# GpSimd scaling of the pooled attention weights, single sums of q and k, and a halved last store in a fused attention and two-layer kernel

## The chip, the cores and the metric

The kernel runs on one core of one Trainium2 chip. A core has five engines with a queue of instructions each: TensorE (PE in the profile, with its weight loads as PEld), VectorE (DVE), ScalarE (ACT), GpSimd (POOL) and SyncE (SP), which here issues all the DMAs. The metric is the time of one execution on the device, in microseconds (us); lower is better.

## The reference

```
# attention, q k v: (4 batches, 8 heads, 576 positions, 64)
q_d, k_d, v_d = means over 4 neighbouring positions            # 144 positions
out_d  = softmax(q_d k_d^T / 8) v_d, each row repeated 4 times  # pooled part
scores = q k^T / 8, kept where |i - j| < 4                      # local part, 7 wide
out    = out_d + softmax(scores) v
x = out as (2304 tokens, 512)
h = x @ w_in;  g = max(h, 0) + alpha * min(h, 0);  x = g @ w_out        # 512 -> 2048 -> 512
h = x @ w_in2; g = where(h > 0, h, exp(min(h, 0)) - 1); y = g @ w_out2  # 512 -> 2048 -> 512
```

All of it is in float32, and the weights of both layers come as float64 bits that the kernel decodes.

## The kernel before

**Tiling.** Two heads make a pair `p`, so a batch `b` has four. Half a batch (288 tokens) is a group, `g` or `u`. The first layer runs over groups and over 16 slices `f` of 128 hidden channels, numbered `s`: `mm_in` multiplies slice `f` of `w_in` (tile `wi`), `th_elem` applies the activation (tiles `n`, `r`, then a high half `gh` and a low half `gl`), and `out1` multiplies by `w_out` (`wo`) into four banks of PSUM. Except in the first six slices, a float32 product is made from three products of high and low halves: the high half of a weight is an ACT copy, the low half a DVE subtraction into the same tile (`raw_l`, `raw_d`). Before that, ACT and DVE decode the bits (`raw_a`, `raw_b`; tiles `cp`, `rawi`, `rawo`, `cw`). The second layer has the same parts in a Strassen form; `th_fin2` adds its last partial sums (tile `os`) and stores rows of 128 tokens.

**Attention of batch 0** comes first, since the first layer needs its output. For each pair: `sums_qk` sums q and k over four positions on DVE, `sums_v` does it for v on POOL (tile `vh`); `sd_mm` forms the pooled scores, `sd_max`, `sd_exp` and `sd_rec` the softmax (tile `P`, row sums `dsum`), `sd_norm` scales `P` by one over the row sums, `pt_mm` and `pt_ev` transpose it, `dav_mm` multiplies by v. The local part is `th_dense` and `th_soft0` (tiles `Dmx`, `Dden`, `dP`; `d_mm` makes the scores, `d_av` multiplies by v), once for each half `u`. `p_add` adds the two into `x`, and when pair `p` of half 0 is there, `mm_first` can multiply its quarter of the sum over 512 channels. While it waits for a quarter of slice 0, it may take the quarters that are there for slices 1 up to `EB` - 1.

**Attention of batches 1 to 3** is spread between the slices of the first layer. `load_qk` brings q and k of a pair, `s_mm` forms the scores of a block (20 blocks, 2 heads), `s_ev` and `s_write` bring them to DRAM (`ss`, `scr`), and once all pairs are written, `s_read` reads the band (`sd`) and `softmax_a` and `softmax_b` run on DVE.

**What sets the order.** The order on each engine is fixed at build time: threads of Python generators (`th_...`) yield what they wait for, each with a priority (`VP`, `DP`, `NP0`, `US`, `OX` and others; a lower one goes first), and a clock inside the program (`_Clock`) decides which one records its next instruction. Where that clock sees TensorE without work, `run_while` records a small multiplication of ones (tile `warm`). So a change of a cost or a priority moves instructions of many other threads. `yield ("DVE",)` hands the turn to other threads until the clock's DVE is near. All instructions are recorded by a helper at L326, so that rows of the profile are told apart by their tiles.

Of the kernel before, what the change touches and what calls it, by code (L numbers as in the profile page):

```python
# [7 lines left out]
F32 = mybir.dt.float32  # L8
# [5 lines left out]
ALU = mybir.AluOpType  # L14
AX = mybir.AxisListType
# [3 lines left out]
S = 576  # L19
D = 64  # L20
NP = H // 2
DM = H * D
# [11 lines left out]
HALO = 3  # L34
# [3 lines left out]
SD = S // 4  # L38
# [7 lines left out]
ZK = 7  # L46
LO = 2
VP = -15.5
DP = -14.5
NP0 = -14.95  # L50
STEP = 1.0
TC = 105
# [2 lines left out]
U2 = G2 // 2  # L55
XR = 11
DN = 1
BIAS = -9000.0
NP2 = NF // 2
WARM = True  # L60
# [16 lines left out]
OSD = 12  # L77
OSO = -4
OAV = 12
OX = -5  # L80
UD = -11
US = -10
UG = (("xcp",3),("xcp",3),("xc",0,0),("xc",0,0))
EB = 2
PSX = 1
PV = 1
VTM = 1
# [243 lines left out]
def fused_kernel(ctx: ExitStack, tc: tile.TileContext, qk, vt, vk, vl, ql, kl, w_in1, w_out1, alpha,  # L331
# [3 lines left out]
    PE, ACT, DVE, SP, POOL = (_Engine(n, e, ck) for n, e in  # L335
                              (("PE", nc.tensor), ("ACT", nc.scalar), ("DVE", nc.vector), ("SP", nc.sync),
                               ("POOL", nc.gpsimd)))
# [7 lines left out]
    accb, hb = bank[0:4], bank[4:6]  # L345
# [15 lines left out]
    osp = dram.tile([NTOK, DM], F32, name="osp")  # L361
# [6 lines left out]
    Ap = pA.__enter__()  # L368

    assert w_in1.dtype == U64  # L370
    WS = 2.0 ** -8
# [110 lines left out]
    st = {}  # L482
# [120 lines left out]
    def sums_qk(b, p):  # L603
        if b:
            sm = Ap.tile([128, 2 if VTM else 3, SD], F32, tag="sm", name="sm", bufs=2)
        else:
            sm = st["qk", 0, p][1][:, SP_:].rearrange("p (a c) -> p a c", a=3)
        st["sm", b, p] = sm
        for a in range(2):
            DVE.tensor_reduce(out=sm[:, a, :],  # L610
                              in_=st["qk", b, p][a][:, HALO:HALO + S].rearrange("p (c f) -> p c f", f=4),
                              axis=AX.X, op=ALU.add)

    def sums_v(b, p):
        if not b and PV:
# [148 lines left out]

    def sd_norm(key, dve):
        P, sm = st[("P",) + key], st.pop(("ds",) + key)
        for r in range(2):
            for i in range(len(key[2])):
                if dve:
                    DVE.tensor_scalar(out=P[:, r, i], in0=P[:, r, i], scalar1=sm[:, r, i], scalar2=None, op0=ALU.mult)  # L770
                else:
                    ACT.activation(out=P[:, r, i], in_=P[:, r, i], func=AF.Copy, scale=sm[:, r, i])
# [101 lines left out]
    NJ = NF // 4  # L874
    NB2 = -(-NTOK // G2)
    HALF = NB2 - 1
    turns = [(1, 0), (2, 1), (0, 2), (3, 3), (1, 4), (HALF, 4), (2, 5), (0, 6), (3, 7), (HALF, 8)]
# [3 lines left out]
    size = [min(G2, NTOK - z * G2) for z in range(NB2)]  # L881
# [23 lines left out]
    def spawn(gen, pri, start=-1, lim=LIM, early=EARLY):  # L905
        threads.append({"g": gen, "p": pri, "s": start, "c": ck.ctx(), "w": None, "l": lim, "e": early})
        threads.sort(key=lambda t: t["p"])

    def finish(*key):
        done[key] = ck.cur["t"]  # L910
# [237 lines left out]
    def th_pair(b, p):  # L1148
        if b:
            if b == 1:  # L1150
                yield "key", *GATE
            yield "tok", "qk"
            yield "tok", "vv"
            yield ("DMA",)
            load_qk(b, p)
            finish("ld", b, p)
            load_v(b, p)
        else:
            yield "key", "ld0", p, 1
        if b:  # L1160
            yield "tok", "sm"
        yield ("DVE",)
        sums_qk(b, p)
        finish("sq", b, p)
        if not b:
            yield "key", "ldv", p
        if b and VTM:
            yield "tok", "vs"
        yield ("DVE",) if b or not PV else ("POOL",)
        sums_v(b, p)  # L1170
        finish("sv", b, p)
        if b:
            put("vv")
            if VTM:
                finish("vs", b, p)
                yield from th_da(b, p, (0, 1))
                return
            yield "tok", "vs"
        bks = yield "bank", 1
        vT_mm(b, p, bks[0])  # L1180
        if not b:
            finish("vT", p)
        yield ("ACT",)
        vT_ev(b, p, bks[0])
        release(bks)
        finish("vs", b, p)
        if b:
            yield from th_da(b, p, (0, 1))

    def th_da(b, p, qs):  # L1190
        key = (b, p, qs)
        yield "tok", "P"
        bks = yield "bank", 2, 1
        sd_mm(b, p, qs, bks)
        if b:
            put("sm")
        if b or not PSX:
            yield ("ACT",)
            sd_ev(key, bks)
            release(bks)  # L1200
            bks = None
        yield ("DVE",)
        sd_max(key, bks)
        yield ("ACT",)
        sd_exp(key, bks)
        if bks:
            release(bks)
        yield ("DVE",)
        sd_rec(key)
        yield ("DVE",) if b < DN else ("ACT",)  # L1210
        sd_norm(key, b < DN)
        yield "tok", "pt"
        bks = yield "bank", 2
        pt_mm(key, bks)
        put("P")
        yield ("ACT",)
        pt_ev(key, bks)
        release(bks)
        if b in QUAD:
            finish("pt", b, p)  # L1220
            return
        yield "key", "vs", b, p
        if b and SPR:
            bks = yield "spare", 1
        else:
            bks = yield "bank", 1
        dav_mm(key, bks[0])
        put("pt")
        if b:
            put("vs")  # L1230
        else:
            finish("dav", p, qs)
        yield ("ACT",)
        dav_ev(key, bks[0])
        (unspare if b and SPR else release)(bks)
        finish("od1", b, p, qs)
        if all(("od1", b, z, qs) in done for z in range(NP)):
            finish("od", b, qs[-1])
# [595 lines left out]
    def down2(u, f):  # L1834
        i, j = divmod(u, NJ)
        z, wq = turns[i]
        wq += j
        run_until("gu", u, f)
        run_until("wo", wq, f)
        gh, gl = gs["u", u]  # L1840
        W2 = st["Wo", wq, f]
        t = [done["gu", u, f], done["wo", wq, f]]
        for m in range(size[z] // 128):
            if not j and not f:
                last = i - 1 if not i or m < size[turns[i - 1][0]] // 128 else i - 2
                run_until("fin2", last, m)
                t.append(done["fin2", last, m])
            at(*t)
            c = f * size[z] + m * 128
            for k, (g, pw) in enumerate(((gh, "h"), (gh, "l"), (gl, "h"))):  # L1850
                PE.matmul(out=accb[m], lhsT=g[:, c:c + 128], rhs=W2[:, HL[pw]],
                          start=(not j and not f and k == 0), stop=(j == NJ - 1 and f == 1 and k == 2))
            if j == NJ - 1 and f:
                spawn(th_fin2(i, m), -101)
            tick()
        if lastv[wq] == i:
            ck.cur["t"] = ck.t["PE"]
            finish("fr", wq // NJ + 1, wslot[wq % NJ][4 + f])
# [9 lines left out]
            st["os", i, m] = t  # L1868
            finish("os", i, m)

    def th_fin2(i, m):
        z, h = turns[i][0], again[i]
        r0 = z * G2 + m * 128
        ck.cur["t"] = ck.t["PE"]
        if h:
            yield "key", "os", i, m
            t = st.pop(("os", i, m))
            yield ("DVE",)
            DVE.scalar_tensor_tensor(out=t, in0=accb[m], scalar=WS, in1=t, op0=ALU.mult, op1=ALU.add)
        else:  # L1880
            yield "tok", "os"
            yield ("ACT",) if m % 2 else ("DVE",)
            t = cp["pool"].tile([128, DM], F32, tag="os", name="os", bufs=4)
            if m % 2:
                ACT.activation(out=t, in_=accb[m], func=AF.Copy, scale=WS)
            else:
                DVE.tensor_scalar(out=t, in0=accb[m], scalar1=WS, scalar2=None, op0=ALU.mult)
        finish("fin2", i, m)
        SP.dma_start(out=(out if h else osp)[r0:r0 + 128, :], in_=t)
        put("os")  # L1890
        if not h:
            finish("part", z, m)
        if all(("fin2", i, k) in done for k in range(size[z] // 128)):
            finish("fin2", i)

    ring = [0]

    with tc.manual_schedule():
        cp["pool"], cp["cw"] = Ap, 2
# [3 lines left out]
        for step in LORD.split():  # L1903
            p = int(step[1:] or 0)
# [27 lines left out]
        for b in range(1, B):  # L1932
            g0 = 32 * (b - 1)
            for z in range(NP):
                p = QORD[z] if b in QUAD else z
# [13 lines left out]
            for u in range(2):  # L1949
                spawn(th_vl(b, u), g0 + 5 + u)  # L1950
                spawn(th_av(b, u), g0 + OAV + 16 * u, -1, LS)
                for i in range(HT // TS):
                    spawn(th_x(b, u, i), g0 + 16 * u + OX + i / 10)
        at(4000.0)
        DVE.tensor_scalar(out=nal, in0=nal, scalar1=-1.0, scalar2=1.0, op0=ALU.mult, op1=ALU.add)
        for s in range(NS1):
            slot[0] = s if s else -1
            ly, g, f, first, last, i = seq[s]
# [3 lines left out]
            if s == TC:  # L1962
# [7 lines left out]
                for q in range(NQ):  # L1970
                    p = 2 + max(0, q - NJ + 1) + q / 100
# [10 lines left out]
            key = (ly, "i", f)  # L1982
            wk = ("w32" if s < F1 else "w", key)
            run_until(*wk)
            if s < F1:
                t = 0.0
            else:
                run_until("xc", *segs[i][4:6])
                t = tm["x"]
# [25 lines left out]
            while len(pend) > LAG or (last and len(pend) > 1) or (first and not seq[pend[0]][5] == i):  # L2015
                z = pend.pop(0)
# [2 lines left out]
                sync()  # L2019
        for m in range(4):  # L2020
            done["fin2", -1, m] = 0.0
        NU2 = len(turns) * NJ
        for u in range(NU2):
            slot[0] = NS1 + u
            i, j = divmod(u, NJ)
# [108 lines left out]
```

## Time and profile before

| | |
|---|---|
| median of 3 runs | 890.29 us (888.11 to 893.06) |
| the profiled execution | 887.87 us |
| its span, first to last instruction | 886.10 us |
| PE busy | 874.3 us, 6631 instructions |
| DVE, ACT, POOL busy | 743.9, 544.9, 4.8 us |
| mean granted clock of TensorE | 0.998 of full speed |

The profiled execution lies 2.42 us below the median, and 1.77 us of it lie outside the span. TensorE is busy nearly throughout, so what counts is the time in which it is idle, runs multiplications of ones, or runs at the lower clock.

### The profile page before, as it was taken

The numbers are of one execution on the slowest core, as the hardware profiler recorded it, in microseconds if no ns is written. First come the engines' busy times: TensorE is split into PE (matmuls) and PEld (weight loads), VectorE is DVE, ScalarE is ACT, GpSimd is POOL, SyncE is SP. The second block draws the span as 40 slices with busy tenths as digits, with TensorE's granted clock in tenths as the row PEclk, the third lists the DMA queues.
The fourth block names the chain that finished last, engine by engine and source line by source line (L and its number), as shares of the span: only waits on it lengthen the run. The fifth ranks groups of instructions, "written<-read, shape, count | busy, mean of one in ns | idle before, by whom it ended". The sixth has DMA issues, their size and how long they took to land.

```text
span 886.1 us, 17496 instructions
## 1 busy us (share of the span) xinstructions
PE 874.3 (99%) x6631; PEld 812.9 (92%) x6631; DVE 743.9 (84%) x1618; ACT 544.9 (61%) x1436; POOL 4.8 (1%) x12
## 2 busy tenths in 40 slices
PE   8999999999999999999999999999999999999998
PEld 6679889999999999999999999999999899999987
DVE  6999899898899989998676999979796669887952
ACT  6899887893447734344365776756565556656643
POOL 2000000000000000000000000000000000000000
PEclk9999999999999999999999999999999999999999
DMA  9958813603405132011402814141414064250501
GB/s 315 344 186 232 256 22 108 187 17 103 126 5 173 41 93 69 1 56 45 163 28 95 265 49 170 48 166 51 141 48 143 2 217 132 83 190 25 191 26 71
DMA packets 67716, 103.80 MB, mean 117 GB/s; under 512 B 26784, under 2 KB 43424, under 8 KB 67632
## 3 DMA queue, kind: packets, MB, share of 16 engines
q1 hardware_dynamic: 67632, 102.68, 36.4%
q8 instruction: 52, 0.85, 0.4%
q14 instruction: 32, 0.26, 0.1%
HBM read 84.75 MB, written 17.92 MB: 116 GB/s over the span
## 4 chain that ended last, share of the span: by engine, by line
PE 87%; DVE 5%; ACT 4%; DMA 2%; issue 1%; SPq 0%; ACTq 0%; DVEq 0%
PE bank L326 87%; ACT P L326 1%; ACT dP L326 1%; DMA rawi<-in_w_in_dram 1%; DMA qk<-in_qk_dram 1%; DVE gl L326 0%; DVE qk L326 0%; ACT cp L326 0%; DMA ident<-in_ident_dram 0%; SPq L326 0%; DVE n L326 0%; DVE wi L326 0%; DVE acc L326 0%; DVE r L326 0%; DMA out_dram<-os 0%
## 5 line engine op out<-in xcount | busy, mean ns | idle before, releaser
L326 PE MATMUL bank<-gh,wo 128*128 128x288 f32 x976 | 221.6, 299 | 0.0
L326 PE MATMUL bank<-xh,wi 128*128 128x288 f32 x976 | 218.3, 298 | 2.0 <-DVE wi L326 2.0
L326 PEld LDWEIGHTS bank<-xq,wi 128*128 128x128 f32 x1536 | 194.4, 191 | 6.1
L326 PE MATMUL bank<-xq,wi 128*128 128x256 f32 x1536 | 196.4, 283 | 0.0
L326 ACT ACTIVATE n<-bank 128x288 f32<-128x288 f32 (+1 forms) x176 | 70.3, 400 | 184.5 <-PE bank L326 179.7
L326 PE MATMUL bank<-wo,gh 128*128 128x512 f32 x576 | 179.3, 392 | 0.0
L326 PEld LDWEIGHTS bank<-xh,wi 128*128 128x128 f32 x976 | 164.2, 189 | 4.4 <-DVE wi L326 2.2
L326 PEld LDWEIGHTS bank<-gh,wo 128*128 128x128 f32 x976 | 165.6, 189 | 2.4 <-issue 2.1
L326 PE MATMUL bank<-gl,wo 128*128 128x288 f32 x488 | 145.3, 298 | 0.2 <-DVE gl L326 0.2
L326 PE MATMUL bank<-xl,wi 128*128 128x288 f32 x488 | 144.2, 295 | 0.0
L326 PEld LDWEIGHTS bank<-wo,gh 128*128 128x128 f32 x576 | 103.1, 189 | 17.5
L326 PE MATMUL bank<-wo,gl 128*128 128x512 f32 x288 | 112.4, 390 | 0.8 <-DVE gl L326 0.7
L326 PEld LDWEIGHTS bank<-gl,wo 128*128 128x128 f32 x488 | 92.2, 189 | 0.5 <-DVE gl L326 0.4
L326 PEld LDWEIGHTS bank<-xl,wi 128*128 128x128 f32 x488 | 92.4, 189 | 0.1
L326 ACT ACTIVATE gh<-r 128x288 fp32r<-128x288 f32 x122 | 53.9, 442 | 54.0 <-DVE r L326 53.5
L326 DVE SCALAR_TENSOR_TENSOR r<-n,nal,bank 128x288 f32<-128x288 f32 x128 | 64.9, 508 | 22.1 <-ACT n L326 21.7
L326 PEld LDWEIGHTS bank<-wo,gl 128*128 128x128 f32 x288 | 54.1, 188 | 13.6 <-DVE gl L326 1.8
L326 DVE TENSOR_TENSOR gl<-r,gh 128x288 fp32r<-128x288 f32 x122 | 55.0, 452 | 8.2 <-ACT gh L326 7.7
L326 DVE TENSOR_TENSOR gl<-n,gh 128x512 fp32r<-128x512 f32 (+1 forms) x80 | 50.2, 633 | 7.1 <-ACT gh L326 6.0
L326 DVE TENSOR_TENSOR c<-m,bank 128x256 f32<-128x256 f32 x64 | 26.3, 418 | 35.1 <-PE bank L326 34.7
L326 ACT ACTIVATE gh<-n 128x512 fp32r<-128x512 f32 (+1 forms) x80 | 46.1, 582 | 13.2 <-DVE n L326 12.9
L326 ACT ACTIVATE n<-n 128x512 f32<-128x512 f32 (+1 forms) x80 | 47.2, 589 | 2.5
(123 smaller groups left out, 1225.3 us busy)
## 6 DMA issues: line engine op xcount, KB each, us to landing
rawo<-in_w_out_dram SPq DMA_DIRECT2D x38, 512.0 KB
rawi<-in_w_in_dram SPq DMA_DIRECT2D x36, 512.0 KB
qk<-in_qk_dram SPq DMA_DIRECT2D x12, 582.0 KB
vl<-in_vl_dram SPq DMA_DIRECT2D x6, 960.0 KB
x<-yT SPq DMA_DIRECT2D x8, 576.0 KB
osp<-os SPq DMA_DIRECT2D x18, 256.0 KB
os<-osp SPq DMA_DIRECT2D x18, 256.0 KB
out_dram<-os SPq DMA_DIRECT2D x18, 256.0 KB
```

The lines of the kernel that those rows point to most:

```text
L326: return fn(*args, **kw)
```

## The change

Seven edits:

- In batch 0, `P` is scaled on POOL: two tensor_tensor multiplications for a pair (72 partitions, 2 x 144 elements), with the two reciprocals of `dsum` broadcast along the row, in place of four DVE tensor_scalar multiplications of 72 x 144.
- `sums_qk` only makes the tile; the sums of k and then of q are two steps with a `yield` ahead of each.
- `EB` is 1: `mm_first` takes no quarters of slice 1 while it waits.
- `DP` (pooled attention of batch 0) goes from -14.5 to -14.7.
- `UG`: the second half of the local part of pairs 0 and 1 waits for quarter 2 of `x`, not quarter 3.
- `OX`: the transposes of the local output of batches 1 to 3 go from -5 to -3.
- The very last row tile is added and stored in two halves of 256 columns.

```
-DP = -14.5
+DP = -14.7
+NG = {0}
+QG = {0: (), 1: (), 2: (), 3: ()}
-OX = -5
+OX = -3
-UG = (("xcp",3),("xcp",3),("xc",0,0),("xc",0,0))
-EB = 2
+UG = (("xcp",2),)*2+(("xc",0,0),)*2
+EB = 1
@@ sums_qk
         st["sm", b, p] = sm
-        for a in range(2):
-            DVE.tensor_reduce(out=sm[:, a, :],
-                              in_=st["qk", b, p][a][:, HALO:HALO + S].rearrange("p (c f) -> p c f", f=4),
-                              axis=AX.X, op=ALU.add)
+    def sum_qk(b, p, a):
+        x = st["qk", b, p][a][:, HALO:HALO + S]
...
+        DVE.tensor_reduce(out=st["sm", b, p][:, a, :], in_=x.rearrange("p (c f) -> p c f", f=4),
+                          axis=AX.X, op=ALU.add)
@@ sd_norm
         P, sm = st[("P",) + key], st.pop(("ds",) + key)
+        if key[0] in NG:
+            for r in range(2):
+                POOL.tensor_tensor(out=P[:, r], in0=P[:, r], in1=sm[:, r].to_broadcast([72, len(key[2]), SD]), op=ALU.mult)
+            return
@@ th_pair
-        yield ("DVE",)
         sums_qk(b, p)
+        for a in (1, 0):
+            yield ("POOL",) if a in QG[b] else ("DVE",)
+            sum_qk(b, p, a)
         finish("sq", b, p)
@@ th_da
-        yield ("DVE",) if b < DN else ("ACT",)
+        yield ("POOL",) if b in NG else ("DVE",) if b < DN else ("ACT",)
         sd_norm(key, b < DN)
@@ down2
+            end = u == NU2 - 1 and f and m == size[z] // 128 - 1
...
-                spawn(th_fin2(i, m), -101)
+                for a in range(2 if end else 1):
+                    cols = slice(a * (DM // 2), (a + 1) * (DM // 2)) if end else slice(0, DM)
+                    spawn(th_fin2(i, m, cols, not end or a), -101)
@@ th_fin2
-            DVE.scalar_tensor_tensor(out=t, in0=accb[m], scalar=WS, in1=t, op0=ALU.mult, op1=ALU.add)
+            DVE.scalar_tensor_tensor(out=t, in0=accb[m][:, cols], scalar=WS, in1=t, op0=ALU.mult, op1=ALU.add)
...
-        SP.dma_start(out=(out if h else osp)[r0:r0 + 128, :], in_=t)
+        SP.dma_start(out=(out if h else osp)[r0:r0 + 128, cols], in_=t)
```

`QG` is empty for every batch, so that no sum of q or k goes to POOL. The multiplications of TensorE are the same in number and form in both programs, but for those of ones: 73 before and 81 now.

First, DVE in the middle of batch 0's pair 0, before (`qk_11` holds the sums of pair 1, `dP_180` is the local part of pair 0, `bank_69` the local scores of pair 1):

```order
L326 TENSOR_TENSOR dP_180<-dP_180,Dden 128x350
L326 TENSOR_REDUCE qk_11_114<-qk_10_113 128x144
L326 TENSOR_REDUCE qk_11_114<-qk_11_114 128x144
L326 TENSOR_SCALAR dsum<-dsum 72x4
L326 RECIPROCAL dsum<-dsum 72x4
L326 TENSOR_SCALAR P<-P,dsum 72x144 x4
L326 TENSOR_REDUCE Dmx<-bank_69 128x5
```

and the same place now:

```order
L328 TENSOR_TENSOR dP_180<-dP_180,Dden 128x350
L328 TENSOR_REDUCE qk_11_114<-qk_11_114 128x144
L328 TENSOR_SCALAR dsum<-dsum 72x4
L328 RECIPROCAL dsum<-dsum 72x4
L328 TENSOR_REDUCE qk_11_114<-qk_10_113 128x144
L328 TENSOR_REDUCE Dmx<-bank_69 128x5
```

The reciprocals move between the two sums, and the four multiplications leave DVE.

Second, TensorE around the local outputs (`dP`, `vd`) of pairs 2 and 3 of batch 0, before (`rawi_290` is slice 0 of `w_in`, `rawi_350` slice 1, `x` the attention's output, `vd_109` with `identb` the mask with which a `d_mm` begins):

```order
L326 MATMUL bank_71<-x,rawi_350 128x288
L326 MATMUL bank_69<-pt,qk_30_129 64x144 x4
L326 MATMUL bank_71<-x,rawi_350 128x288
L326 MATMUL bank_72<-dP_452,vd_139 64x64 x8
L326 MATMUL bank_72<-dP_452,vd_139 64x32 x2
L326 MATMUL bank_71<-x,rawi_350 128x288
L326 MATMUL bank_70<-x,rawi_290 128x288
L326 LDWEIGHTS identb
L326 MATMUL bank_73<-vd_109,identb 128x350
L326 MATMUL bank_73<-qk_01_106,qk_00_105 64x70 x10
```

and now, where slice 0 is `rawi_278` and slice 1 `rawi_330`, from pair 2's output to the second half of pair 0 and, behind the dots, from pair 3's output:

```order
L328 MATMUL bank_66<-dP_326,vd_135 64x64 x8
L328 MATMUL bank_66<-dP_326,vd_135 64x32 x2
L328 LDWEIGHTS warm
L328 MATMUL bank_71<-warm 128x224
L328 MATMUL bank_70<-x,rawi_278 128x288
L328 LDWEIGHTS identb
L328 MATMUL bank_73<-vd_109,identb 128x350
L328 MATMUL bank_73<-qk_01_106,qk_00_105 64x70 x10
...
L328 MATMUL bank_66<-dP_426,vd_139 64x64 x8
L328 MATMUL bank_66<-dP_426,vd_139 64x32 x2
L328 MATMUL bank_70<-x,rawi_278 128x288
L328 MATMUL bank_71<-x,rawi_330 128x288
```

Slice 1 no longer stands between pair 3's output and the last quarter of slice 0; the second halves of pairs 0 and 1 have moved ahead of pair 3's output.

## Rows read from the trace of the kernel before

**Rows 1.** Page, section 1: busy us, share of span, instructions.
```profile
PE 874.3 (99%) x6631; PEld 812.9 (92%) x6631; DVE 743.9 (84%) x1618; ACT 544.9 (61%) x1436; POOL 4.8 (1%) x12
```
**Rows 2.** Waits of PE: us in total, times, longest.
```profile
PE bank L326 <- DVE wi L326: 2.0, 1, 2.0
...
PE bank L326 <- DMA qk<-in_qk_dram: 0.9, 1, 0.9
```
**Rows 3.** Windows: stretch, then busy us of each engine, clock, DMA, GB/s.
```profile
12.00:32.00 20.00, 19.36 (x251) 15.26 (x246) 18.89 (x62) 17.52 (x81) 3.45 (x6) 1.00 1.02 370
...
80.00:130.00 50.00, 46.87 (x434) 43.52 (x433) 45.17 (x99) 41.90 (x122) 0.00 (x0) 0.97 0.60 161
130.00:420.00 290.00, 289.79 (x2391) 284.16 (x2390) 266.62 (x600) 162.66 (x536) 0.00 (x0) 1.00 0.27 77
```
**Rows 4.** Timeline of PE, end of batch 0's attention: start, us, what, idle before.
```profile
25.72 1.15 PE L326 MATMUL bank<-warm 128*128 128x224 bf16 x10
26.80 0.72 PE L326 MATMUL bank<-pt,qk 72*64 72x144 f32 x8
...
31.99 0.75 PE L326 MATMUL bank<-x,rawi 128*128 128x288 f32 x2 [0.64 <-DVE rawi L326]
...
34.00 0.78 PE L326 MATMUL bank<-dP,vd 70*64 70x64 f32 x20
34.71 1.39 PE L326 MATMUL bank<-x,rawi 128*128 128x288 f32 x4
35.93 0.31 PE L326 MATMUL bank<-vd,identb 128*128 128x350 bf16 x1
...
36.93 0.75 PE L326 MATMUL bank<-x,rawi 128*128 128x288 f32 x2
```
**Rows 5.** Timeline of DVE, batch 0.
```profile
12.27 1.46 DVE L326 TENSOR_SCALAR P<-P,dsum 72x144 f32<-72x144 f32 x4
...
29.82 0.45 DVE L326 TENSOR_TENSOR x<-bank,od 128x288 f32<-128x288 f32 x1
```
**Rows 6.** Tile P, batch 0: ns min/median/max, first and last start.
```profile
L326 DVE TENSOR_SCALAR P<-P,dsum x16: 280/284/681, 12.3 to 29.1; 72x144 f32<-72x144 f32 x16
```
**Rows 7.** Timeline of POOL, batch 0, pair 1.
```profile
12.20 0.67 POOL L326 TENSOR_TENSOR vh<-v 128x288 f32<-128x288 f32 x1 [2.05 <-DMA v<-in_vt_dram]
12.94 0.50 POOL L326 TENSOR_TENSOR qk<-vh 128x144 f32<-128x144 f32 x1
```
**Rows 8.** Timeline of PE and SP, batch 1, pairs 2 and 3.
```profile
91.57 0.84 PE L326 MATMUL bank<-qk 64*64 64x70 f32 x40 [0.28 <-ACT gh L326]
...
96.80 0.55 SPq L326 DMA_DIRECT2D qk<-in_qk_dram  x1
...
102.47 0.85 PE L326 MATMUL bank<-qk 64*64 64x70 f32 x40 [0.87 <-DMA qk<-in_qk_dram]
```
**Rows 9.** Timeline of DVE and PE, around the softmax of batch 1.
```profile
116.70 0.51 DVE L326 SCALAR_TENSOR_TENSOR r<-n,nal,bank 128x288 f32<-128x288 f32 x1 [0.81 <-ACT n L326]
...
121.26 0.29 PE L326 MATMUL bank<-xh,wi 128*128 128x288 f32 x1
121.39 0.29 PE L326 MATMUL bank<-xl,wi 128*128 128x288 f32 x1
...
122.92 0.68 DVE L326 TENSOR_TENSOR wi<-cw,wi 128x512 fp32r<-128x512 f32 x1
...
123.66 0.65 PE L326 MATMUL bank<-xh,wi 128*128 128x288 f32 x2 [1.97 <-DVE wi L326]
```
**Rows 10.** Windows behind that wait; the clock is the third number from the end.
```profile
124.00:125.00 1.00, 1.00 (x6) 1.00 (x5) 1.00 (x2) 0.24 (x1) 0.00 (x0) 0.50 0.08 16
...
127.00:128.00 1.00, 1.00 (x8) 1.00 (x8) 1.00 (x3) 0.02 (x1) 0.00 (x0) 0.83 0.03 8
```
**Rows 11.** Timeline of DVE and SP, the last two stores.
```profile
881.75 1.37 DVE L326 SCALAR_TENSOR_TENSOR os<-bank,os 128x512 f32<-128x512 f32 x2 [1.23 <-PE bank L326]
...
882.46 1.02 SPq L326 DMA_DIRECT2D out_dram<-os  x2
```

More of the change, by code (lines that the diff above doesn't have):

```diff
@@ L608, in sums_qk @@
         st["sm", b, p] = sm
-        for a in range(2):
-            DVE.tensor_reduce(out=sm[:, a, :],
-                              in_=st["qk", b, p][a][:, HALO:HALO + S].rearrange("p (c f) -> p c f", f=4),
-                              axis=AX.X, op=ALU.add)
+    def sum_qk(b, p, a):
+        x = st["qk", b, p][a][:, HALO:HALO + S]
+        if a in QG[b]:
+            x = x.rearrange("p (n c) -> p n c", c=2)
+            h = Ap.tile([128, S // 2], F32, tag="pa", name="qh", bufs=2)
+            POOL.tensor_tensor(out=h, in0=x[:, :, 0], in1=x[:, :, 1], op=ALU.add)
+            h = h.rearrange("p (n c) -> p n c", c=2)
+            POOL.tensor_tensor(out=st["sm", b, p][:, a, :], in0=h[:, :, 0], in1=h[:, :, 1], op=ALU.add)
+            return
+        DVE.tensor_reduce(out=st["sm", b, p][:, a, :], in_=x.rearrange("p (c f) -> p c f", f=4),
+                          axis=AX.X, op=ALU.add)
     def sums_v(b, p):
@@ L766, in sd_norm @@
         P, sm = st[("P",) + key], st.pop(("ds",) + key)
+        if key[0] in NG:
+            for r in range(2):
+                POOL.tensor_tensor(out=P[:, r], in0=P[:, r], in1=sm[:, r].to_broadcast([72, len(key[2]), SD]), op=ALU.mult)
+            return
         for r in range(2):
@@ L1869, in th_os, with th_fin2 @@
             finish("os", i, m)
-    def th_fin2(i, m):
+    def th_fin2(i, m, cols, last):
         z, h = turns[i][0], again[i]
@@ L1876, in th_fin2 @@
             yield "key", "os", i, m
-            t = st.pop(("os", i, m))
+            t = st["os", i, m][:, cols]
             yield ("DVE",)
-            DVE.scalar_tensor_tensor(out=t, in0=accb[m], scalar=WS, in1=t, op0=ALU.mult, op1=ALU.add)
+            DVE.scalar_tensor_tensor(out=t, in0=accb[m][:, cols], scalar=WS, in1=t, op0=ALU.mult, op1=ALU.add)
         else:
@@ L1887, in th_fin2 @@
                 DVE.tensor_scalar(out=t, in0=accb[m], scalar1=WS, scalar2=None, op0=ALU.mult)
-        finish("fin2", i, m)
-        SP.dma_start(out=(out if h else osp)[r0:r0 + 128, :], in_=t)
+        if last:
+            finish("fin2", i, m)
+        SP.dma_start(out=(out if h else osp)[r0:r0 + 128, cols], in_=t)
+        if not last:
+            return
         put("os")
@@ L1896, in fused_kernel @@
     ring = [0]
+    NU2 = len(turns) * NJ
     with tc.manual_schedule():
@@ L2021, in fused_kernel @@
             done["fin2", -1, m] = 0.0
-        NU2 = len(turns) * NJ
         for u in range(NU2):
```

## The prediction

> **What bounds the kernel.** I read the totals first: TensorE is busy for 874.3 us of a span of 886.1 us [rows 1]. Then the list of what TensorE waited for, where the longest single wait is 2.0 us for the low half of a weight (`wi`) from DVE and the next that this change can touch is 0.9 us for q and k from DRAM [rows 2]. Then the stretches: from 130 to 420 us TensorE idles for 0.2 us, but from 80 to 130 us it is busy for 46.87 of 50 us at a mean clock of 0.97 [rows 3]. Last the timeline of the head, because up to 32 us TensorE is filled up with multiplications of ones [rows 4]. DVE and ACT are both nearly full there, 18.89 and 17.52 of 20 us [rows 3].
>
> Both programs have the same useful multiplications. So the time can differ only by the ones, by TensorE's idle time, by time at the lower clock, and by the last store. I sum these four, against the profiled execution of 887.87 us; it lies 2.42 us below the median of 890.29, and I put the difference on the median.
>
> **The ones.** 81 in place of 73. Ten of them take from 25.72 to 26.80, 0.108 us each [rows 4]. All of the additional ones stand in the head, where TensorE goes through its queue in order and cannot drop them: 8 x 0.108 = **+0.9 us**. They would cost nothing where TensorE would have waited anyway; that is the lower end, 0.
>
> **Quarters 2 and 3 of slice 0.** Each needs, behind the local output `d_av` of its pair, the DVE addition into `x`, 0.45 us [rows 5], and two handovers between engines; one of them is 0.06 us from the end of `wi` at 123.60 to TensorE's start at 123.66 [rows 9]. That is 0.57 us at least; I take 0.7. Before, quarters of slice 1 filled this gap: `d_av` at 34.00 is followed at 34.71 without a break [rows 4]. With `EB` = 1 nothing stands there for pair 3 and a single one (0.11) for pair 2, so 0.7 + 0.6 = 1.3 us of idle come in. The 0.64 us at 31.99, where a quarter of slice 1 waited for its weight [rows 4], go. Net **+0.7 us**. The ends are +0.4 (handovers of 0.06) and +1.7, as pair 2's addition stands on DVE behind the decoding of a weight that ACT hands over late. The two second halves of the local part that come earlier take 1.0 us each (35.93 to 36.93, [rows 4]) and are useful work that is then missing later; they move and cost nothing.
>
> **Scaling on POOL.** DVE loses 16 multiplications of median 284 ns [rows 6], some 4.5 us. POOL gets 8 of 288 columns. The trace has none with a broadcast operand; the nearest row is the addition of 128 x 288 at 0.67 us [rows 7]. So a pair takes 2 x 0.67 = 1.3 us in place of about 1.1. For pair 0 the reciprocals end about 11.7 us, half a microsecond earlier than before, since one sum of q and k now stands behind them; POOL is done at about 13.2. TensorE comes to the transposes at about 13.7, behind the pooled scores of pair 1 and five ones. So POOL is hidden there, and I take 0. If the cover of 0.5 us is gone, each pair pays what is over. The ends are -1.0 (TensorE's small waits in the head shrink as DVE is freed) and +2.7 (four pairs at 0.67 more). I do not expect the 4.5 us to come back: behind DVE, ACT is late next with 17.52 of 20 us [rows 3], and the ones in TensorE's queue were laid out for this pace.
>
> **The order of the two sums** is 0 by itself; it gives the half microsecond used above. `DP` and `UG` are in the count of ones and the order already.
>
> **q and k of batch 1.** A pair's load is issued behind the stores of the pair before, so from one pair's block scores to the arrival of the next pair's q and k there is a chain: from 91.57 to 102.47, 10.9 us, and TensorE, with 51 multiplications of 288 columns and the pooled ones in between, was ready 0.87 earlier [rows 8]. Now 66 such multiplications stand between pairs 2 and 3. At 0.13 us each (121.26 to 121.39, [rows 9]) that is 2.0 us more, and the wait goes: **-0.9 us**. But between pairs 1 and 2 there are now 57, without the 8 transposes of `P` (0.6 us): 10.0 + 6 x 0.13 - 0.6 = 10.2 us against a chain of 10.9. A wait of up to 0.7 can come; I take half, **+0.4 us**, ends 0 and 0.7.
>
> **The low half of `wi`.** The softmax of batch 1 stands on DVE between `r` at 116.70 and `wi` at 122.92, and TensorE idles 1.97 us for it [rows 9]. In the new order a weight's low half and one decoding step (0.68 and some 0.4 us) stand ahead of `r`, where DVE idled 0.81 us for ACT [rows 9]. The gain is between 0 (DVE is then late for `r`) and 0.81; following DVE's queue from the slice before, it comes to `r` about as late as now, so I take half, **-0.4 us**. 1.6 us of waiting remain. Behind the wait the granted clock is 0.50, which is 1.2 GHz, until into the slice 127 to 128 (0.83) [rows 10]; 3.3 us at half speed lose about 1.7. I leave that as it is.
>
> **The last store.** Two adds end 1.37 us after 881.75 and their two issues take 1.02 us together [rows 11]. The second half of the tile is added when the whole one was, at about 883.1, and its issue may stand behind the first half's (0.5 us); only its transfer is shorter. Between -0.35 (half of an add) and +0.3: **-0.1 us**.
>
> **Sum.** 0.9 + 0.7 + 0 - 0.9 + 0.4 - 0.4 - 0.1 = +0.6 us: 888.5 for the profiled execution and 890.9 for the median. About 0.5%, 4.5 us, is what a measurement of this kernel can tell from no change.
>
> **Rivals.**
>
> *The clock stays up.* The wait for `wi` falls by the full 0.81, the clock is not lowered, and pair 2 does not wait: 0.4 + 1.7 + 0.4 = 2.5 us less, 888.4. For it: the wait shrinks, and other waits of under 1 us left no trace in the clock (1.00 from 12 to 32 us, [rows 3], with the 0.64 of [rows 4] in it). Against it: 1.2 us and more remain, in a stretch where DVE is full, 45.17 of 50 [rows 3]. Chance 0.22.
>
> *GpSimd's scaling sets the head (slower).* If a broadcast operand doubles an instruction to 1.3 us, a pair takes 2.7 in place of 1.1, the cover of 0.5 is gone from 1.8 us a pair on, and the transposes of pairs 2 and 3, the last ones, wait 0.9 to 1.4 us each; such idle time next to the gaps at quarters 2 and 3 reaches the 1.97 us behind which the clock fell [rows 9, 10]. 2 x 1.4 + 1.7 = 4.5 us more, 895.4. For it: no row has such an instruction. Against it: POOL's rows grow with the columns, 144 at 0.50 and 288 at 0.67 [rows 7], and the number of columns read stays. Chance 0.10.
>
> *POOL and DVE get in each other's way.* When POOL added at 12.20 [rows 7], DVE's first scaling at 12.27 took 1.46 us for four [rows 5], and one of the 16 took 681 ns, against a median of 284 [rows 6]. Now POOL's scaling of pair 3 meets a weight's decoding on DVE, an instruction of the same kind, which stands ahead of the addition for quarter 2: up to one POOL instruction, 0.67, on the path. 891.6. Chance 0.13. The Trainium skill ("SBUF — State Buffer", section "SBUF: two separate sides") says that DVE and GpSimd share a pair of ports as an exclusive lock, held for a whole instruction, against a DVE instruction in a two-port mode or with two SBUF inputs. The trace agrees, with the 681 ns above; by the rule this rival is the forecast, by the medians it is not.
>
> *A new wait later.* The order differs until about 420 us, and DVE has 266.62 of 290 us there [rows 3]. One more wait of 2 us with its clock is 1.97 + 1.7 = 3.7 us, 894.6. Chance 0.08; before there is 0.2 us of idle in that stretch.
>
> **How the numbers follow.** My forecast has 0.47. Its own range, from the ends above and the runs' spread of about 2.5 us either way, is 888 to 894. With the clock rival below and the two slower ones above, 8 in 10 lie between 886.8 and 894.8. Below 885.8 (faster by 0.5%) lie a part of the clock rival and gains in the head that I have not seen, 0.08; above 894.7 lie most of the GpSimd rival and half of the later wait, 0.11; the rest is 0.81.
>
> **What would show it.** 81 multiplications of ones; no wait for q and k ahead of pair 3 of batch 1 and perhaps one ahead of pair 2; gaps of some 0.7 us ahead of quarters 2 and 3 of slice 0; POOL instructions of 72 x 288 at about 0.67 us; a wait for `wi` of about 1.6 us with a slice of low clock behind it. POOL at 1.3 us, transposes of `P` that wait for POOL, or a clock that stays at 1.00 would make it wrong, as would a head that ends more than 1 us earlier.

## The result, and the profile after

The changed kernel is slower: 895.93 us (median of 14 runs, 891.28 to 898.97) against 890.18 us (14 runs, 887.83 to 893.06), a ratio of 1.0067 with an interval of 1.0053 to 1.0082. That is 6 us, above the range of the prediction.

Its profiled execution took 892.94 us, 5.07 us more than that of before, and is one of the quicker of its kind: the mean granted clock was 0.997 in it, and between 0.989 and 0.999 in the 14 runs, with a median of 0.9945. The kernel before has a median of 0.997 or 0.998 wherever it ran beside the experiments below. The difference, 0.0025 to 0.0035 of 890 us, is an estimate of 2.2 to 3.1 us, so some two fifths to a half of the 6 us is clock.

First the totals and the longest waits of TensorE (in all, times, longest) after the change. They answer to [rows 1, 2].

```profile
PE 875.5 (98%) x6639; PEld 813.0 (91%) x6639; DVE 743.4 (83%) x1603; ACT 544.2 (61%) x1436; POOL 10.4 (1%) x20
```

```profile
PE bank L328 <- DMA qk<-in_qk_dram: 3.9, 3, 1.6
PE bank L328 <- DVE x L328: 2.1, 2, 1.5
PE bank L328 <- DVE wi L328: 1.9, 2, 1.6
```

Waits for q and k, and for `x`, have come in at the top of the list, and the one for `wi` has stayed. (Of the 3.9 us for q and k, 1.04 are batch 0's own load, ahead of 8.89 us.) The same stretches as in [rows 3], after the change:

```profile
12.00:32.00 20.00, 19.36 (x253) 15.18 (x251) 15.55 (x43) 17.92 (x80) 7.02 (x12) 1.00 1.02 372
80.00:130.00 50.00, 45.48 (x464) 41.67 (x462) 43.51 (x94) 39.95 (x115) 0.00 (x0) 1.00 0.73 189
130.00:420.00 290.00, 289.25 (x2382) 283.14 (x2383) 268.81 (x601) 164.88 (x542) 0.00 (x0) 1.00 0.27 76
```

DVE did lose 3.3 us from 12 to 32 us, and TensorE gained nothing by it. From 80 to 130 us TensorE is idle for 4.5 us where it was 3.1.

Next the end of batch 0's attention on TensorE, as in [rows 4]: pair 2's local output, the one multiplication of ones, quarter 2, and at the bottom pair 3's output and the last quarter.

```profile
30.38 0.78 PE L328 MATMUL bank<-dP,vd 70*64 70x64 f32 x20
31.09 0.27 PE L328 MATMUL bank<-warm 128*128 128x224 bf16 x1
32.86 1.33 PE L328 MATMUL bank<-x,rawi 128*128 128x288 f32 x2 [1.50 <-DVE x L328]
...
38.92 0.78 PE L328 MATMUL bank<-dP,vd 70*64 70x64 f32 x20
40.33 1.24 PE L328 MATMUL bank<-x,rawi 128*128 128x288 f32 x4 [0.63 <-DVE x L328]
```

The gap ahead of the last quarter is 0.63 us, as worked out; the one ahead of quarter 2 is 1.50. DVE at that moment (the decoding step `cp`, undisturbed at the top and then ahead of the addition), and POOL (scaling of pair 2, undisturbed, and of pair 3):

```profile
29.29 0.42 DVE L328 TENSOR_SCALAR cp<-cp 128x512 uint32<-128x512 uint32 x1
...
31.60 0.84 DVE L328 TENSOR_SCALAR cp<-cp 128x512 uint32<-128x512 uint32 x1 [0.28 <-ACT cp L328]
32.36 0.45 DVE L328 TENSOR_TENSOR x<-bank,od 128x288 f32<-128x288 f32 x1
```

```profile
25.09 1.29 POOL L328 TENSOR_TENSOR P<-P,dsum 72x288 f32<-72x288 f32 x2 [3.60 <-DVE dsum L328]
31.49 1.47 POOL L328 TENSOR_TENSOR P<-P,dsum 72x288 f32<-72x288 f32 x2 [5.11 <-DVE dsum L328]
```

The addition stands behind a step that first waits for ACT and then takes 0.84 us in place of 0.42, while POOL scales `P`, itself 0.18 us slower than for pair 2. The Trainium skill ("SBUF — State Buffer", section "SBUF: two separate sides") has the two engines block each other for whole instructions over a shared pair of ports; these rows agree. Behind the gap the clock falls to 1.2 GHz (third number from the end):

```profile
32.00:33.00 1.00, 0.14 (x1) 0.14 (x1) 1.00 (x3) 0.12 (x1) 0.96 (x2) 0.88 1.01 218
33.00:34.00 1.00, 1.00 (x3) 0.51 (x3) 0.97 (x3) 0.46 (x1) 0.00 (x0) 0.50 1.08 247
...
36.00:37.00 1.00, 1.00 (x17) 0.80 (x17) 0.00 (x0) 0.52 (x2) 0.00 (x0) 0.91 0.87 290
```

Then batch 1. TensorE's block scores of pairs 1, 2 and 3 after the change, and SyncE's issues between them, to be held against [rows 8]:

```profile
86.16 0.85 PE L328 MATMUL bank<-qk 64*64 64x70 f32 x40 [1.57 <-DMA qk<-in_qk_dram]
...
97.83 0.85 PE L328 MATMUL bank<-qk 64*64 64x70 f32 x40 [1.33 <-DMA qk<-in_qk_dram]
...
109.74 0.85 PE L328 MATMUL bank<-qk 64*64 64x70 f32 x40
```

```profile
68.53 2.68 SPq L328 DMA_DIRECT2D scr<-ss  x4
...
75.12 2.46 SPq L328 DMA_DIRECT2D yT0a<-ys  x4
...
79.06 0.43 SPq L328 DMA_DIRECT2D qk<-in_qk_dram  x1
...
87.54 2.88 SPq L328 DMA_DIRECT2D scr<-ss  x4
90.52 0.55 SPq L328 DMA_DIRECT2D qk<-in_qk_dram  x1
```

and SyncE's issues in the kernel before, for the load of pair 1 and the stores of pair 0:

```profile
65.75 0.43 SPq L326 DMA_DIRECT2D qk<-in_qk_dram  x1
...
74.44 2.68 SPq L326 DMA_DIRECT2D scr<-ss  x4
```

Before, the load of pair 1 was issued ahead of the stores of pair 0 (its scores began at 77.29 without a wait). Now it stands behind these stores, the stores of `ys` and three weights, and is issued 13 us later, while pair 0's scores are only 3.6 us later (66.53, 62.91 before). TensorE waits for it. The low half of `wi` and the last stores, which answer to [rows 9, 11]:

```profile
130.02 0.53 PE L328 MATMUL bank<-xh,wi 128*128 128x288 f32 x2 [1.64 <-DVE wi L328]
```

```profile
886.87 1.44 DVE L328 SCALAR_TENSOR_TENSOR os<-bank,os 128x512 f32<-128x512 f32 x3 [1.23 <-PE bank L328]
...
887.59 1.31 SPq L328 DMA_DIRECT2D out_dram<-os  x3
```

From the first of these additions to the end of the span it is 4.33 us, and was 4.35.

The 5.07 us of the two profiled executions, from TensorE's waits of 0.2 us and more, its ones and its clock:

| | before | after | difference |
|---|---|---|---|
| waits from 5 to 12 us | 2.38 | 2.94 | +0.56 |
| ones (by count, 0.108 us each) | 73 | 81 | +0.9 |
| ahead of quarters of `x` (31.99; 32.86, 40.33) | 0.64 | 2.13 | +1.49 |
| ahead of block scores of batch 1 | 1.15 | 2.90 | +1.75 |
| `wi` (123.66; 130.02, 133.69) | 1.97 | 1.87 | -0.10 |
| others from 140 to 420 us | 0.21 | 0.39 | +0.18 |
| time lost to the low clock | 1.7 | 1.7 | 0 |

That is 4.8 us; where the other 0.3 lie is not shown. The first row is mere variation: the same instructions waited 1.63 us in the run e5_noend below and 3.41 in e1_qk.

### The profile page after: what moved, and what is told of

The parts are those of the page before. It is cut to its first block, busy times and chain, and to the rows that moved or that the text cites. A ratio compares the mean times of both kernels' runs of the same rounds, so it can differ in the third digit from the quotient of the medians.

```text
span 891.2 us, 17514 instructions
## 1 busy us (share of the span) xinstructions
PE 875.5 (98%) x6639; PEld 813.0 (91%) x6639; DVE 743.4 (83%) x1603; ACT 544.2 (61%) x1436; POOL 10.4 (1%) x20
## 4 chain that ended last, share of the span: by engine, by line
PE 84%; ACT 6%; DVE 5%; DMA 3%; issue 1%; SPq 1%; POOL 0%; DVEq 0%; ACTq 0%
PE bank L328 84%; DMA qk<-in_qk_dram 2%; ACT dP L328 1%; ACT cp L328 1%; ACT P L328 1%; DMA v<-in_vt_dram 1%; ACT cw L328 1%; DMA rawo<-in_w_out_dram 1%; ACT wo L328 1%; DMA vl<-in_vl_dram 1%; ACT wi L328 1%; SPq L328 1%; ACT n L328 0%; DVE xl L328 0%; DVE acc L328 0%
```

## The experiments

Three theories could carry the 6 us. A: the waits for q and k, by the place of the loads in SyncE's queue. B: the head, with the gap at quarter 2. C: the low clock behind such gaps, which hits some executions and not others. D and E are the two causes of the gap, GpSimd and the decoding step. Of the seven edits, `DP` and `OX` by themselves leave the program of either kernel as it is, so they had no run; the sums given out singly had none of their own. The ratios are to the kernel before on the same chip, with their intervals; the clock is the median over the executions.

| run | median us | ratio | clock |
|---|---|---|---|
| the change | 895.93 | 1.0067 (1.0053 to 1.0082) | 0.9945 |
| e1_qk | 889.55 | 1.0012 (0.9990 to 1.0034) | 0.998 |
| e2_ones | 891.55 | 1.0020 (1.0007 to 1.0033) | 1.000 |
| e3_dve | 896.55 | 1.0069 (1.0048 to 1.0090) | 0.993 |
| e5_noend | 897.54 | 1.0081 (1.0062 to 1.0101) | 0.992 |
| e7_step | 893.60 | 1.0054 (1.0034 to 1.0075) | 0.9965 |
| e9_q2ones | 892.12 | 1.0037 (1.0025 to 1.0050) | 0.997 |
| e10_all | 888.42 | 0.9996 (0.9983 to 1.0008) | 1.000 |
| e6_bng | 907.05 | 1.0196 (1.0173 to 1.0219) | 0.989 |
| e13_bebug | 898.31 | 1.0109 (1.0083 to 1.0136) | 0.995 |
| e14_aebug | 897.42 | 1.0090 (1.0072 to 1.0108) | 0.994 |
| e11_bpool | 889.49 | 1.0015 (0.9997 to 1.0033) | 0.998 |
| e12_bbest | 886.78 | 0.9975 (0.9963 to 0.9987) | 0.999 |

**e1_qk, the loads of q and k.**

```
     def s_write(b, p, t):
+        preload(b, p + 1)      # b == 1: load_qk's tile and its DMA, here
```

> The changed kernel, with q and k of pairs 1 to 3 of batch 1 loaded ahead of the four stores of the pair before them in SyncE's queue; every other engine's instructions stay as they were. Theory A (the loss comes from the two waits for q and k): the waits of 1.57 and 1.33 us ahead of pairs 1 and 2 go, nothing takes their place, and the time is 2.9 us lower, about 893.0, ratio to the kernel before 1.003. Theory B (the loss is the head of the program, up to 42 us, and the low clock behind its gaps): the waits may go, but the stretch behind them gives the time back (the wait for wi grows), ratio still 1.006.

889.55 us: about 5 us of the 6 are gone (between 2.6 and 7.2 with both intervals), by three DMAs moved in one queue. SyncE's issues around pair 0 and TensorE's scores of pairs 1 to 3 in this run:

```profile
71.32 0.43 SPq L586 DMA_DIRECT2D qk<-in_qk_dram  x1
73.84 2.69 SPq L328 DMA_DIRECT2D scr<-ss  x4
```

```profile
90.21 0.85 PE L328 MATMUL bank<-qk 64*64 64x70 f32 x40
...
100.48 0.85 PE L328 MATMUL bank<-qk 64*64 64x70 f32 x40
...
112.40 0.85 PE L328 MATMUL bank<-qk 64*64 64x70 f32 x40
```

No wait is left at any of them (the times are later since this execution ran at the low clock from 11 to 15 and from 35 to 48 us). Theory A holds, and B's rival that something later gives the time back falls. The gain is above the 2.9 us of the two waits, though theory A's ratio of 1.003 lies in the interval; the median clock went from 0.9945 to 0.998 with them. That the loads are the cause of this second part is not shown. The gap at quarter 2 is 1.50 us in this run too, and the moved loads act only behind 70 us; yet clocks of 0.992 and less, as in the profiles with the long low stretch behind quarter 2, came in 2 of 12 executions here, in 5 of 14 of the changed kernel and in 5 of 6 of e5_noend.

**e2_ones and e9_q2ones, ones in the gaps.**

```
+            if kt == 2: ones(hb[1][:, G1:512], 13)                    # both runs
+        ones(bks[0], {(1, 1): 13, (1, 2): 11}.get((b, p), 0))         # e2_ones
+                ones(hb[s % 2][:, G1:512], 14 if s == 20 else 0)      # e2_ones
```

> The changed kernel, with 13 multiplications of ones ahead of quarter 2 of slice 0, 13 and 11 ahead of the block scores of pairs 1 and 2 of batch 1, and 14 ahead of the slice whose low half of wi is late, at 0.108 us each: as much as TensorE waited there. All other instructions stay. Theory C (idle gaps of 1.3 to 1.6 us lower the clock behind them, not each one in each execution): the mean granted clock is 0.999 or more in every execution, the slice at 0.50 behind quarter 2 goes, and the time falls by 1.7 us in the profile and by 3 to 4 us in the median, ratio 1.002 to 1.004. If the clock has no part in the difference, the time stays at 1.0067 or rises by up to 0.5 us where a wait was shorter than its ones.

> The changed kernel, with 13 multiplications of ones ahead of quarter 2 of slice 0 alone. Useful work comes no earlier by it. If the clock behind quarter 2 is the cost, the wait is filled, the clock stays up to 46 us, and the time falls by as much as the low clock took, 1.7 us in a short stretch and 6 us in a long one: ratio 1.002 to 1.004. If the idle time itself is the cost, the ratio stays at 1.006 to 1.007.

Work that computes nothing made the kernel faster: by 2.7 us with quarter 2's gap filled alone, by 4.2 with four gaps. The two gains have intervals of 1.0 to 4.4 and 2.4 to 5.9 us. In e2_ones the clock is 0.998 to 1.000 in all executions (0.999 or more was expected). Theory C holds: both ratios lie below 1.006. The stretch from 33 to 46 us, first in e5_noend, where that gap is as in the changed kernel, then in e2_ones:

```profile
33.00:46.00 13.00, 12.37 (x111) 8.90 (x110) 7.44 (x19) 6.98 (x29) 0.00 (x0) 0.51 0.64 191
```

```profile
33.00:46.00 13.00, 12.37 (x150) 9.20 (x149) 10.98 (x30) 10.43 (x50) 0.00 (x0) 1.00 0.97 289
```

At the low clock TensorE gets through 111 multiplications in place of 150. From the start of quarter 2 to pair 0's block scores it takes 37.92 us (32.47 to 70.39) in place of 32.17 (32.34 to 64.51), so 5.75 us are lost. In the changed kernel's profile, by the same measure, it is 1.50 us (32.86 to 66.53), for the same 1.50 us of waiting. Part of what the filled gap wins is given back at pair 1, whose load still stands behind the stores (e2_ones):

```profile
85.08 0.84 PE L328 MATMUL bank<-qk 64*64 64x70 f32 x40 [1.23 <-DMA qk<-in_qk_dram]
```

Here 13 ones and 1.23 us of waiting replace the changed kernel's 1.57.

**e3_dve, the scaling given to DVE at the same places.**

```
+    DVEP = _Engine("POOL", nc.vector, ck)    # POOL for the planner, DVE on the chip
-                POOL.tensor_tensor(out=P[:, r], in0=P[:, r], in1=sm[:, r]...
+                DVEP.tensor_tensor(out=P[:, r], in0=P[:, r], in1=sm[:, r]...
```

> The changed kernel, with the eight scalings of the pooled weights of batch 0 given to VectorE in place of GpSimd, at the same places of the order, nothing else moved. Theory D (GpSimd's scaling of pair 3 holds up the weight decoding on VectorE ahead of quarter 2): that decoding step takes 0.42 instead of 0.84 us, the wait ahead of quarter 2 falls from 1.50 to about 1.1 us, and the low clock behind it may go: 0.4 to 2 us less. Against it: VectorE now does 8 x 0.4 us itself, so the head may be as late as before: no change.

No change in the time. DVE and TensorE around quarter 2 in this run:

```profile
33.97 0.43 DVE L328 TENSOR_SCALAR cp<-cp 128x512 uint32<-128x512 uint32 x1 [0.35 <-ACT cp L328]
34.31 0.82 DVE L328 TENSOR_TENSOR P<-P,dsum 72x288 f32<-72x288 f32 x2
35.05 0.45 DVE L328 TENSOR_TENSOR x<-bank,od 128x288 f32<-128x288 f32 x1
```

```profile
35.55 1.33 PE L328 MATMUL bank<-x,rawi 128*128 128x288 f32 x2 [1.82 <-DVE x L328]
```

The step is back at 0.43 us, so POOL was what held it up. But DVE's own scaling then stands ahead of the addition, and the wait is longer. Theory D is right on the 0.4 us and wrong as an account of the loss.

**e7_step, the decoding step behind the addition.** The step's instruction is held back in `raw_b` and given out at the end of `p_add`:

```
+        if (b, p, u) == (0, 2, 0):
+            h = held.pop()
+            nc.vector.tensor_scalar(out=h, in0=h, scalar1=3, scalar2=None, op0=ALU.logical_shift_left)
```

> The changed kernel, with two instructions of VectorE in the other order: the addition into x for quarter 2 ahead of the weight's decoding step that waited for ACT and then for GpSimd. Nothing else moves. Theory E (the wait of 1.50 us ahead of quarter 2 is this step, and the low clock behind it is what the executions pay): the wait falls to about 0.5 us, the clock stays at 1.00 from 32 to 46 us, and the median falls by 4 to 6 us, ratio 1.000 to 1.003. If the waits for q and k are what lowers the clock in most executions, the step brings 1 us and the ratio stays at 1.005 or above.

DVE and TensorE in this run:

```profile
32.37 0.46 DVE L328 TENSOR_TENSOR x<-bank,od 128x288 f32<-128x288 f32 x1
32.75 0.79 DVE L702 TENSOR_SCALAR cp<-cp 128x512 uint32<-128x512 uint32 x1
```

```profile
32.88 0.75 PE L328 MATMUL bank<-x,rawi 128*128 128x288 f32 x2 [0.43 <-DVE x L328]
...
85.06 0.84 PE L328 MATMUL bank<-qk 64*64 64x70 f32 x40 [1.89 <-ACT gh L328]
```

The wait falls from 1.50 to 0.43, and the clock stays up there: on the gap theory E is right. Its 4 to 6 us did not come: the median falls by about 1 us, the interval meets that of the changed kernel, and the ratio is what E's alternative gave. At pair 1 TensorE waits 1.89 us in place of 1.57, and this time the clock fell behind it (0.50 from 87 to 89 us). The row names ACT's `gh`, but that ends at 85.07, after TensorE has started; in e10_all ACT's order is the same, only the load stands earlier, and no wait is there. The load moves with the head, though: it is issued at 77.52, 1.54 us earlier than in the changed kernel, pair 0's scores start 1.47 us earlier (65.06), and at pair 1 1.10 us of that is left. So A and B mostly add up, and the head's delay does not hide behind the load's. In this execution the clock was also low from 11 to 15 us; why the median gains so little is not shown.

**e10_all, the three together**: e1_qk, e7_step, 4 ones at quarter 2 and 14 ahead of the late `wi`.

```
+            if kt == 2: ones(hb[1][:, G1:512], 4)
+                ones(hb[s % 2][:, G1:512], 14 if s == 20 else 0)
```

> The changed kernel with all that the runs before point to: the addition for quarter 2 ahead of the decoding step, q and k of batch 1 loaded ahead of the stores, 4 multiplications of ones ahead of quarter 2, and 14 ahead of the slice whose low half of wi is late. Sum of what the rows show: from 892.9 us of the profiled execution 1.0 us of the wait at quarter 2, 1.7 us of its low clock and 2.9 us of the waits for q and k come off, 0.2 us of ones are added: 887.5 us, ratio to the kernel before 0.997 to 0.999, with the clock at 0.999 or more.

888.42 us, the time of before (0.9983 to 1.0008), some 6 us below the changed kernel. The ratio of 0.9996 lies just above the 0.997 to 0.999 that was expected, and the clock was between 0.997 and 1.000, not at 0.999 or more throughout. Quarter 2 and the scores of pair 1 in this run:

```profile
32.20 0.56 PE L914 MATMUL bank<-warm 128*128 128x224 bf16 x4
32.79 0.75 PE L328 MATMUL bank<-x,rawi 128*128 128x288 f32 x2
...
82.99 0.85 PE L328 MATMUL bank<-qk 64*64 64x70 f32 x40
```

So loads, gap and clock together carry the loss. How it divides among them is not settled: e1_qk alone brings back some 5 us and e9_q2ones 2.7, more than the 6 there are.

**e5_noend, the last tile whole**, by the flag that makes the halves:

```
-            end = u == NU2 - 1 and f and m == size[z] // 128 - 1
+            end = False and u == NU2 - 1 and f and m == size[z] // 128 - 1
```

> The changed kernel, with the last tile stored whole as before. By the forecast the halves are worth 0.1 us (between -0.3 and 0.35): the same time within the measurement.

1.0081 against 1.0067, intervals that overlap: the halves are worth nothing that shows.

**The parts of the change alone.** e6_bng is before with the scaling on GpSimd, e13_bebug before with `EB` = 1 and the new `UG`, e14_aebug the changed kernel with `EB` and `UG` of before. In all three the planner lays out an order of its own.

```
+        if not key[0]: two POOL.tensor_tensor as in the change, and return      # e6_bng
-EB = 2                                                                          # e13_bebug
+EB = 1
-UG = (("xcp",3),("xcp",3),("xc",0,0),("xc",0,0))
+UG = (("xcp",2),)*2+(("xc",0,0),)*2
-EB = 1                                                                          # e14_aebug
+EB = 2
-UG = (("xcp",2),)*2+(("xc",0,0),)*2
+UG = (("xcp",3),("xcp",3),("xc",0,0),("xc",0,0))
```

> The kernel before, with one part of the change alone: the pooled weights of batch 0 scaled by GpSimd with broadcast sums. The planner then lays out its own order. If GpSimd's scaling is a cost by itself (contention with VectorE, or slower scaling), this is slower than before by 0.3% or more; if the loss comes from the order with EB = 1 and the new UG, it stays within 0.3% of before.

> The kernel before, with EB = 1 and the new UG alone; the planner lays out its own order for these. If the quarters of slice 1 that no longer fill the gaps of slice 0 are the cost, this is slower than before by 0.3% or more, with a wait for x ahead of a quarter of slice 0 and a low clock behind it. If it is within 0.2%, EB and UG cost only together with the scaling on GpSimd.

> The changed kernel with EB and UG of before: scaling on GpSimd, sums given out singly, halves at the end. With the run of the kernel before that had the scaling on GpSimd alone (1.020) it tells what the sums given out singly are worth in that order. If every new order brings its own waits, it is slower than before, by 0.3 to 2%; if EB = 1 was the cost, it is within 0.3% of before.

e6_bng and e13_bebug are slower than the whole change; the interval of e14_aebug meets it. e14_aebug differs from e6_bng by the sums given out singly, the halves at the end, `DP` and `OX`, and is about 1% faster; that this is owed to the single sums is likely and not shown. The longest waits of the three are not of the edited operations; the longest two of e13_bebug, and the longest of e6_bng with SyncE's issues ahead of it:

```profile
81.00 1.44 PE L326 MATMUL bank<-qk 64*64 64x70 f32 x40 [2.15 <-DMA qk<-in_qk_dram]
...
174.01 0.40 PE L326 MATMUL bank<-gh,wo 128*128 128x288 f32 x1 [2.22 <-ACT gh L326]
```

```profile
76.58 2.71 SPq L326 DMA_DIRECT2D scr<-ss  x4
...
87.56 0.33 SPq L326 DMA_DIRECT2D qk<-in_qk_dram  x1
```

```profile
96.92 0.84 PE L326 MATMUL bank<-qk 64*64 64x70 f32 x40 [3.76 <-DMA qk<-in_qk_dram]
```

In all three the load of pair 1 stands behind pair 0's stores and those of `ys`, as in the changed kernel, and pair 1's scores wait for it: 3.76 us in e6_bng, 2.15 in e13_bebug, 2.61 in e14_aebug. In e13_bebug TensorE waits 0.56 us for `x` ahead of a quarter, and the clock stays at 1.00 from 30 to 50 us; the low clock that was expected behind it did not come in this execution.

By these runs alone GpSimd's scaling would be a cost of 2%. The next one keeps the order.

**e11_bpool, GpSimd's scaling in the order of before.** The planner goes on counting DVE's 16 multiplications, which are not given out:

```
+        if not key[0]:
+            for r in range(2):
+                nc.gpsimd.tensor_tensor(out=P[:, r], in0=P[:, r], in1=sm[:, r].to_broadcast(...), op=ALU.mult)
-                    DVE.tensor_scalar(out=P[:, r, i], ...
+                    (DVE if key[0] else DVEN).tensor_scalar(out=P[:, r, i], ...
```

> The kernel before, with the 16 scalings of the pooled weights of batch 0 on VectorE replaced by eight of GpSimd with broadcast sums, at the same places; all else stays in the order of before (the planner still counts them as VectorE's). This is the scaling on GpSimd by itself, without a new order. Theory F (the scaling itself is free, the order around it costs): within 0.2% of before. Rival (GpSimd's scaling slows the head by itself): the transposes of P wait longer or VectorE's decoding steps are held up, 1 us or more, ratio 1.002 or above.

1.0015 with 1.000 in the interval: by itself the scaling costs nothing that shows, and 3 us at most. The contention is there too, DVE's step beside POOL's scaling of pair 3 in this run:

```profile
30.18 0.92 DVE L326 TENSOR_SCALAR cp<-cp 128x512 uint32<-128x512 uint32 x1 [0.83 <-ACT cp L326]
```

but the quarters of slice 1 stand in front of quarter 2 of slice 0, and TensorE does not wait for `x`; its wait for a weight of slice 1 is 0.91 us, against 0.64 before. So most of the 2% of e6_bng is its new order.

**e12_bbest, what was learned put into the kernel before**: the loads as in e1_qk, 17 ones ahead of the late `wi`.

```
     def s_write(b, p, t):
+        preload(b, p + 1)
...
+                ones(hb[s % 2][:, G1:512], 17 if s == 20 else 0)
```

> The kernel before, with q and k of batch 1 loaded ahead of the stores and 17 multiplications of ones ahead of the slice whose low half of wi is late. By the rows of before the wait of 0.87 us and the low clock of 1.7 us go: 2.6 us less, ratio 0.997, and it would be faster than both kernels. If only executions with a low clock gain by the ones, 1 to 2 us less.

886.78 us, 2.2 us faster than before and faster than both kernels. The scores of batch 1 no longer wait, and ahead of `wi`:

```profile
120.10 1.85 PE L884 MATMUL bank<-warm 128*128 128x224 bf16 x17
...
122.44 0.53 PE L326 MATMUL bank<-xh,wi 128*128 128x288 f32 x2 [0.21 <-DVE wi L326]
```

## Why the prediction was wrong

- **q and k of batch 1** is the step that failed: -0.9 and +0.4 were forecast, and the waits went up by 1.75 us. The first half was right: pair 3 does not wait. Between pairs 1 and 2 the work of TensorE was right as well (10.3 us of the 11.67 between the two starts, 10.2 forecast), but the chain had been taken at before's 10.9 us and took 11.67, with 7.3 us from the load's issue at 90.52 to its use, against 5.7 in [rows 8]. And the wait ahead of pair 1 is not in the forecast at all: its sentence that a load is issued behind the stores of the pair before is not true of pair 1 in the kernel before (65.75, ahead of the stores at 74.44) and became true with the change (79.06, behind those at 68.53). I followed two pairs and did not look where the first load had gone in SyncE's queue. By e1_qk this step is some 5 us of the 6; the 2.9 us of the two waits are in the rows, the rest came with a higher clock.
- **The clock** was left as it was behind `wi` and put nowhere else. It was not lowered behind `wi` this time (1.00 from 130 us on) but behind quarter 2, and in other profiles for longer (e5_noend) or in more places (at 11 to 15 us too in e1_qk, e3_dve and e7_step). The forecast worked from one execution, and two fifths to a half of the difference is in how much the clock falls.
- **Quarters 2 and 3**: +0.7 forecast, +1.49 measured, inside the range of 0.4 to 1.7. Quarter 3 was exact (0.63 against 0.7); quarter 2 was at the end that named the decoding step. With that end I had to see 1.5 us of idle in one piece, near the 1.97 behind which the clock had fallen before, and did not price it.
- **POOL and DVE in each other's way**, a rival: it happened (0.84 for 0.42 us), at the place that it named. It is 0.4 us of the gap and alone brings nothing back.
- **GpSimd's scaling sets the head**, the slow rival, gave 895.4, near the measured time, by a mechanism that was not there: two instructions take 1.29 us, 0.65 each, as the forecast's own term has them, and TensorE's transposes of `P` do not wait for POOL.
- **A new wait later** had the right kind of thing, at the wrong place: from 130 to 420 us TensorE has 0.75 us of idle in place of 0.21, and the new waits lie at 33 to 98.
- **The ones** (81, +0.9 by count), **the scaling** (0, by e11_bpool within its interval) and **the last store** (0 for -0.1) were as forecast. Of **the low half of `wi`** 1.64 us are left, as forecast (1.6), but a second wait of 0.23 us follows at 133.69, so -0.1 came in place of -0.4.

Open: why the same gap of 1.50 us is followed by some 3.4 us at the low clock in one execution and by 13 in another, and in some executions of e1_qk (clock 1.000 over all) by none that shows. Open too: which of the edits moved the load of pair 1 behind the stores; each of the three partial orders has it there.

## What to carry to other kernels

Where a build-time planner lays out the order, a change is worth what its new order is worth: keep the order by telling the planner of the old cost, and try the operation by itself, before calling it slow. For each load that a waiting engine needs, look up what now stands ahead of it in the issuing queue, above all stores that wait for something themselves. And an idle gap of 1.5 us on TensorE is to be priced with the clock behind it, over several executions, not from one profile.

## What the runs showed of the hardware

- A broadcast operand costs GpSimd nothing that shows: 72 x 288 took 0.65 us in pairs, beside 0.67 for the 128 x 288 addition without one in [rows 7].
- Behind a wait of 1.50 us the granted clock was 0.50 (1.2 GHz) for 3.4 us or for 13, which put TensorE back by 1.5 or by 5.75 us, with the same work behind the wait. Not every such wait does it: 1.57 and 1.33 us in the changed kernel and 2.05 and 1.59 us in e9_q2ones, ahead of block scores, left the clock at 1.00, while 1.19 to 1.28 us, for POOL's sums of v at 10 to 11 us, were followed by a clock of 0.50 in e1_qk, e3_dve and e7_step.
- Multiplications of ones in a gap, 1.45 us for 13, kept the clock up behind it (1.00 from 33 to 46 us in e2_ones and e9_q2ones) and paid for themselves where useful work had to wait anyway.
